# Attention and two expert mixtures on one core: second products of experts 1 to 4 of the first mixture in float32, straight from the staged weights

## The chip, the cores and the metric

The kernel runs on one core of a Trainium2 chip. Its time is the device time of one execution in microseconds (us). The comparison is the median of several runs of the kernel before and of the changed kernel on the same chip. The engines are named as the profile names them: PE is the matrix engine, PEld its weight loads, DVE the vector engine, ACT the activation engine, POOL the general engine (GpSimd), SP the queue that issues most transfers.

## The reference, cut to what matters

```python
def _moe_ref(x, w_gate, w1, w2):              # first mixture: N=3072, D=512, E=8, F=1024
    cap = N // E                              # 384 tokens for each expert
    logits = x @ w_gate
    # tokens are assigned greedily, the largest logit first, until an expert is full
    for e in range(E):
        mask = assigned == e
        h = np.maximum(x[mask] @ w1[e], 0.0)  # first product
        out[mask] = h @ w2[e]                 # second product
def reference(...):
    x = attention(q, k, v, mem_k, mem_v)      # local windows, 3072 tokens of 512
    x = _moe_ref(x, ...)                      # first mixture
    return _moe2_ref(x, ...)                  # second mixture: top 2 of 8 experts, noisy gate
```

## The kernel before, in words

After the attention the first mixture runs expert by expert. Two things go on at once. **The routing** decides which tokens an expert gets. It is a search, digit by digit, for the logit at which an expert is full, and each digit is a round trip between DVE and PE: DVE compares all tokens with some thresholds (tile `GE`), PE counts (`rps<-OH,GE`), DVE masks the counts (`blk`), PE adds them up (`rps<-blk,same`), DVE sums and compares with the capacity (`sums`, `flt`), PE sums the flags (`rps<-flt,onesb`), and DVE makes the next thresholds (`d`, `ci`, `GE`). One such round trip is called a pass below. An expert takes 8 passes and a closing part (`NQ`, `at`, `exc`, then the list of its tokens, `l1pos` and `slps`). **The experts** whose lists are ready are multiplied on PE in between. PE and DVE run their instructions in program order, and a planner (`Pipe`, with its own costs of instructions) has fixed that order when the program was built: routing products stand among the expert products.

An expert's tokens are gathered by POOL's indirect transfers (`xg<-xr,idx`) and transposed (`xT`). The first product (`mm1`) has 8 groups of 12 matmuls of 384 columns. Its weights come as float32 into staging tiles `st` (4 tiles of 128x1024 for each matrix, 8 buffers in all) and are split into float16 halves, a high and a low part: ACT takes squares for a scale (`junk<-st`) and writes the high part (`w_0h` to `w_3h`), and the low part (`w_0l` to `w_3l`) is made in `halves`, either by DVE in pieces of 256 columns or by POOL in pieces of 512 with two instructions (`st<-st,s`, then `w_0l<-st,w_0h`). The function asks DVE first (`fits`) and takes POOL when DVE has no room in the plan and POOL is idle (`idle`). Three float16 products stand for one product of float32. The rectified result of the first product is split likewise: ACT writes it twice (`ht` in float32, `hT` in float16) and POOL, or DVE, subtracts (`halve`, `hT<-ht,hT`). The second product (`mm2`) then takes 72 matmuls of 512 columns.

Expert 0 alone is done otherwise. ACT writes `hT` once, in float32, with the inverse scale of the first weights (`i1c`), and `mm2_f32` multiplies it with the staged float32 weights themselves: 48 matmuls of 256 columns in float32 into `m2f`. Its second weights are not split.

The transfers of weights are issued by SP in the order of `loads`: w1 of expert 0, w2 of expert 0, w1 of expert 1, and so on. Index i in the code is 2k for w1 and 2k+1 for w2 of expert k; experts 8 to 15 are those of the second mixture. `splits` takes the staged matrices in the same order. While a tile is in use its buffer can't be loaded again.

Of the kernel before, what the change touches and what calls it, by code (L numbers as in the profile page):

```python
# [25 lines left out]
KT, FT = DM // 128, FF // 128  # L26
# [948 lines left out]


C_H = 2.0**-15
SLACKG = -200.0

METAS = 8000.0  # L980
# [1 line left out]
SLACKH = 500.0  # L982


def loads(ctx):

    nc, pipe, t = ctx.nc, ctx.pipe, ctx.t
    for i in range(4 * E):
        k, m = i // 2, i % 2
        if k < E:  # L990
            yield lambda: k in ctx.est_known and (i < 2 or i == 3 or i - 2 in ctx.split)
            if m == 0:
                ev = pipe.D.value_load(ctx.est[0:1, k : k + 1], min_val=0, max_val=E - 1)
            elif k == 0:
                yield lambda: 0 in ctx.gathered
        else:
            yield lambda: i - 2 in ctx.split and (k == E or 1 in ctx.X2 and ctx.ordered)
            if m == 0 and k > E:
                ev = pipe.D.value_load(ctx.perm[0:1, k - E : k - E + 1], min_val=0, max_val=E - 1)
        if k < E:  # L1000
            yield ctx.split.get(i - 2, 0.0)
        else:
            pipe.t["y"] = max(pipe.t["y"], ctx.split[i - 2])
        got = ctx.st[i] = []
        for j in range(4):
            if i == 3:
                yield lambda: ctx.w2_read > 2 * j + 1
            st = ctx.stg.tile([128, 1024], F32, tag="st", name=f"st{i}_{j}", bufs=8)
            src = ((t.w1, t.w2) if k < E else (t.x1, t.x2))[m]
            if k == E:  # L1010
                src = src[0, j]
            else:
                src = src.rearrange("e j p n -> e p j n")[ds(ev, 1), :, j].rearrange("a p n -> (a p) n")
            pipe.D.dma_start(st, src)
            got.append(st)


def splits(ctx):

    for i in range(4 * E):
        if i == 1:
            continue
        yield lambda: i in ctx.st
        yield from split(ctx, i, ctx.st.pop(i), i == 0)


def split(ctx, i, st, eager):
    wp, pipe = ctx.wp, ctx.pipe
    V_, S_, G_ = pipe.V, pipe.S, pipe.G
    k, m = i // 2, i % 2
    W = ctx.W.setdefault(k, {"w1": [], "w2": []})

    def tl(n, shape=(128, 4), dt=F32, **kw):
        return wp.tile(list(shape), dt, tag=n, name=f"{n}_{i}", **kw)

    sq = tl("sq")  # L1040
    sqb = sq.bitcast(BF16).rearrange("p (j h) -> p j h", h=2)[:, :, 1]
    if m == 0:
        W["s1"], W["i1"] = tl("s1", dt=I32, bufs=3).bitcast(F32), tl("i1", dt=I32, bufs=3).bitcast(F32)
        if i == 0:
            W["i1c"] = tl("i1c", bufs=1)

    def after(x):
        return pipe.rdy("v", x) - 100

    def norms(js):  # L1050
        n = js.stop - js.start
        yield pipe.rdy("p", sq) + 1000
        tot = ctx.ms.tile([128, n], F32, tag="mso", name=f"tot{i}")
        pipe.P.matmul(tot, ctx.onesb, sqb[:, js], start=True, stop=True)
        t = tl("nt", dt=I32, bufs=1)
        yield pipe.rdy("v", tot) - 100
        V_.tensor_scalar(
            t[:, js], tot.bitcast(I32), 24, 23, op0=ALU.logical_shift_right, op1=ALU.logical_shift_left
        )
        yield after(t)  # L1060
        i2 = W["i1"] if m == 0 else tl("i2", dt=I32, bufs=1).bitcast(F32)
        V_.tensor_scalar(
            i2[:, js].bitcast(I32), t[:, js], float(23 << 23), float(50 << 23), op0=ALU.max, op1=ALU.add
        )
        if m == 0:
            yield after(i2)
            V_.tensor_scalar(
                W["s1"][:, js].bitcast(I32), i2[:, js].bitcast(I32), -1.0, float(254 << 23), op0=ALU.mult, op1=ALU.add
            )
            if i == 0:  # L1070
                V_.tensor_scalar(W["i1c"][:, js], W["i1"][:, js], C_H, None, op0=ALU.mult)
            return W["s1"]
        yield after(i2)
        q = tl("nq", dt=I32, bufs=1)
        V_.scalar_tensor_tensor(
            q, W["s1"].bitcast(I32), float(127 << 23), i2.bitcast(I32), op0=ALU.add, op1=ALU.subtract
        )
        yield after(q)
        kk = tl("kk", (128, 1), bufs=1)
        V_.tensor_reduce(kk, q.bitcast(F32), axis=AX.X, op=ALU.min)  # L1080
        yield after(kk)
        s2 = tl("s2")
        V_.tensor_scalar(s2, W["i1"], kk, None, op0=ALU.mult)
        comb = tl("comb", (128, 1), I32, bufs=3)
        V_.tensor_scalar(comb, kk.bitcast(I32), -1.0, float(254 << 23), op0=ALU.mult, op1=ALU.add)
        W["comb"] = comb.bitcast(F32)
        return s2

    def halves(j, s):
        done = W["w1" if m == 0 else "w2"]  # L1090
        n = 4 * (i - (i > 1)) + j
        yield lambda: ctx.wnext == n < len(ctx.wfree)
        ctx.wnext += 1
        hi, lo = (wp.tile([128, 1024], F16, tag=f"w{o}", name=f"w{i}_{j}{o}", bufs=12) for o in "hl")
        src = st[j]
        sj = s[:, j : j + 1]
        yield max(pipe.t["s"] - 100, pipe.rdy("s", s))
        pipe.t["s"] = max(pipe.t["s"], ctx.wfree[n] + 200)
        S_.activation(hi, src, AF.Copy, scale=sj)
        yield pipe.rdy("v", hi)  # L1100
        yield lambda: len(done) == j
        fits = pipe.fits(395.0)
        idle = lambda: k <= E and pipe.t["g"] <= pipe.clock + SLACKG
        a = 0
        while a < 1024:
            yield lambda: fits() or idle()
            b = a + 256 if fits() else min(a + 512, 1024)
            if b == a + 256:
                V_.scalar_tensor_tensor(lo[:, a:b], src[:, a:b], sj, hi[:, a:b], op0=ALU.mult, op1=ALU.subtract)
            else:  # L1110
                G_.tensor_scalar(src[:, a:b], src[:, a:b], sj, 1.0, op0=ALU.mult, op1=ALU.mult)
                G_.tensor_tensor(lo[:, a:b], src[:, a:b], hi[:, a:b], op=ALU.subtract)
            a = b
        kn = KT if m == 0 else 2
        hi, lo = (w.rearrange("p (k f) -> p k f", k=kn) for w in (hi, lo))
        done.append((hi, lo))
        if j == 3:
            ctx.split[i] = pipe.rdy("y", lo)

    for j in range(4):  # L1120
        if i == 0 and j > 1:
            yield lambda: 0 in ctx.X1
        yield lambda j=j: len(st) > j
        yield max(pipe.rdy("s", st[j]), pipe.t["s"] - 100)
        junk = ctx.junk.tile([128, 1024], F16, tag="junk", name=f"junk{i}_{j}")
        S_.activation(junk, st[j], AF.Square, accum_out=sq[:, j : j + 1])
        if eager:
            s = yield from norms(slice(j, j + 1))
            pipe.add(halves(j, s))
    if not eager:  # L1130
        s = yield from norms(slice(0, 4))
        if k < E:
            for j in reversed(range(4)):
                pipe.add(halves(j, s), True)
        else:
            for j in range(4):
                yield from halves(j, s)
# [15 lines left out]
def mm1(ctx, k, xT, n, ps, last=True):  # L1153

    pipe, W, hT = ctx.pipe, ctx.W[k], []
    for ft in range(FT):
# [15 lines left out]
                if i < 3 * KT:  # L1172
                    pipe.tick()
        h = ctx.hp.tile([128, 2, XN], F16, tag="hT", name="hT", bufs=FT + 1)
        if k == 0:
            h = h.rearrange("p o n -> p (o n)").bitcast(F32)[:, :n]
            pipe.S.activation(h, ps, AF.Relu, scale=W["i1c"][:, ft // 2 : ft // 2 + 1])
            hT.append(h)
# [37 lines left out]
    return ps  # L1216


def mm2_f32(ctx, hT):

    pipe = ctx.pipe
    ps = [ctx.m1.tile([128, DM], F32, tag="m1", name="m2f") for _ in range(CAP // 128)]
    pipe.until(lambda: 1 in ctx.st)
    for ft in range(FT):
        w2 = ctx.st[1][ft // 2].rearrange("p (k f) -> p k f", k=2)[:, ft % 2]
        pipe.wait(w2, hT[ft])
        for a in range(CAP // 128):
            for n in range(0, DM, DM // 2):
# [2 lines left out]
                    start=(ft == 0 and n == 0), stop=(ft == FT - 1 and n > 0),  # L1231
                )
                pipe.tick()
        ctx.w2_read = ft + 1
    ctx.split[1] = pipe.t["p"]
    return ps


# [160 lines left out]
def moe1(ctx):  # L1399
# [39 lines left out]
    for k in range(E):  # L1439
# [3 lines left out]
        hT = mm1(ctx, k, xT, CAP, ps)  # L1443
        m1_done.add(k)
        ys = ctx.wk.tile([128, NA], F32, tag="ys", name=f"ys{k}")
        if k:
            pipe.until(lambda: "comb" in ctx.W[k])
            pipe.V.tensor_scalar(ys, ix, ctx.W[k]["comb"], 1.0 / C_H, op0=ALU.mult, op1=ALU.mult)
        else:
            pipe.V.tensor_scalar(ys, ix, 1.0 / C_H, None, op0=ALU.mult)  # L1450
            f32 = mm2_f32(ctx, hT)
        for a in range(NA):
            ps = mm2(ctx, k, hT, 128 * a, last=a == NA - 1) if k else f32[a]
            y = ctx.xp.tile([128, DM], F32, tag="pv", name=f"y{k}{a}", bufs=8)
            pipe.S.activation(y, ps, AF.Copy, scale=ys[:, a : a + 1])
            ctx.Y[k, a] = y
# [244 lines left out]
def overflow(ctx):  # L1701
# [8 lines left out]
    with tc.For_i(0, total, 1):  # L1710
# [62 lines left out]
        ev = nc.sync.value_load(ei, min_val=0, max_val=E - 1)  # L1773
        k = 2 * E
        ctx.W.pop(k, None)
        ctx.wfree, ctx.wnext = [0.0] * (8 * (k + 1)), 8 * k - 4
        st = [[], []]
        for m, src in enumerate((t.x1, t.x2)):
            for j in range(4):
# [191 lines left out]
```

## Time and profile before

| | |
|---|---|
| median of 3 runs | 1163.11 us (1149.09 to 1164.64) |
| the profiled execution | 1158.95 us, of which its span 1157.1 us |
| PE busy | 993.3 us (86% of the span) |
| DVE busy | 777.3 us (67%) |
| ACT busy | 536.2 us (46%) |
| POOL busy | 566.4 us (49%) |
| mean granted clock of PE | 0.935 |

The span is the time from the first to the last instruction of the profiled execution; its own time lies 1.9 us above. A busy PE is not a PE at its peak: its records overlap, and a record is longer at a lower granted clock. The attention takes the first 190 us or so, the first mixture the next 390, the second mixture the rest.

### The profile page before, as it was taken

What the parts mean: (1) busy time and instruction counts of PE and PEld (TensorE: products, weight loads), DVE (VectorE), ACT (ScalarE), POOL (GpSimd) and SP (SyncE); (2) the same over time, 40 slices, a digit from 0 to 9 for tenths busy, and PEclk for the clock granted to TensorE, in tenths of its full rate; (3) what the DMA queues carried; (4) which work ended last, traced back from release to release, by engine and by line L of the source; (5) the groups of instructions that cost most, each with busy time, mean ns of one, the idle gap of its engine ahead of it and who ended that gap; (6) DMA issues with size and microseconds to landing.
All of it is one profiled execution on the core that took longest, in us unless ns stands there. A gap on an engine that the chain in (4) does not pass through costs nothing. (4 is left out here: it accounts for less than half of the span.)

```text
span 1157.1 us, 22131 instructions
## 1 busy us (share of the span) xinstructions
PE 993.3 (86%) x7959; PEld 556.4 (48%) x7959; DVE 777.3 (67%) x2352; ACT 536.2 (46%) x958; POOL 566.4 (49%) x690
## 2 busy tenths in 40 slices
PE   6677837987797888867978998999999999999995
PEld 6555635653343344433434554445455454555552
DVE  3576777879988989989677574654747365584100
ACT  2454514455564645667540862525536163553220
POOL 5455614436655656655553452544645445454531
PEclk9898857999997988989889998999999999999998
DMA  9999715528554554996524863665737476543410
GB/s 220 220 261 264 190 52 199 180 96 220 168 154 164 130 195 102 244 263 172 101 58 108 256 194 132 186 187 164 192 105 220 94 189 180 149 112 97 116 49 28
DMA packets 162660, 185.46 MB, mean 160 GB/s; under 512 B 108224, under 2 KB 120896, under 8 KB 162546
## 3 DMA queue, kind: packets, MB, share of 16 engines
q1 hardware_dynamic: 143856, 127.96, 42.5%
q0 software_dynamic: 15232, 49.75, 14.4%
q10 hardware_dynamic: 3458, 6.30, 1.5%
q8 instruction: 64, 1.05, 0.4%
q14 instruction: 50, 0.41, 0.1%
HBM read 127.14 MB, written 32.44 MB: 138 GB/s over the span
## 5 line engine op out<-in xcount | busy, mean ns | idle before, releaser
L68 PEld LDWEIGHTS <-hT 128*128 128x128 f16 (+2 forms) x2088 | 168.8, 99 | 196.9 <-issue 20.1
L68 ACT ACTIVATE ht<-m 128x384 f32<-128x384 f32 (+2 forms) x184 | 91.8, 499 | 330.8 <-PE m L68 302.0
L68 POOL TENSOR_TENSOR hT<-ht,hT 128x384 f16<-128x384 f32 (+2 forms) x154 | 153.3, 1007 | 134.4 <-ACT hT L68 122.1
L68 ACT ACTIVATE junk<-st 128x1024 f16<-128x1024 f32 x124 | 130.9, 1055 | 58.3 <-DMA st<-w_dram 31.3
L68 POOL DMA_INDIRECT out_dram<-pv,ts x47 | 47.1, 1003 | 179.2 <-DVE pv L68 117.8
L68 DVE SCALAR_TENSOR_TENSOR pv<-m,ys,pv 128x512 f32<-128x512 f32 (+2 forms) x47 | 33.5, 713 | 139.2 <-PE m L68 138.8
L68 PE MATMUL m<-xT,w_0h 128*128 128x384 f16 (+2 forms) x384 | 99.7, 339 | 3.3 <-DMA xT<-xg 3.3
L68 PE MATMUL m<-xT,w_1h 128*128 128x384 f16 (+2 forms) x384 | 102.5, 348 | 0.0
L68 PE MATMUL m<-xT,w_3h 128*128 128x384 f16 (+2 forms) x384 | 101.8, 344 | 0.0
L68 PE MATMUL m<-xT,w_2h 128*128 128x384 f16 (+2 forms) x384 | 99.3, 341 | 2.7 <-ACT hT L68 2.7
L68 PE MATMUL m<-w_3h,hT 128*128 128x512 f16 (+2 forms) x348 | 88.8, 353 | 5.6 <-POOL hT L68 5.6
L68 ACT ACTIVATE hT<-m 128x384 f16<-128x384 f32 (+2 forms) x184 | 91.4, 497 | 0.0
L68 PE MATMUL m<-w_0h,hT 128*128 128x512 f16 (+2 forms) x348 | 89.0, 360 | 0.0
L68 PE MATMUL m<-w_1h,hT 128*128 128x512 f16 (+2 forms) x348 | 87.9, 352 | 0.0
L68 PE MATMUL m<-w_2h,hT 128*128 128x512 f16 (+2 forms) x348 | 87.6, 350 | 0.0
L68 POOL TENSOR_SCALAR st<-st,s 128x512 f32<-128x512 f32 x63 | 53.9, 855 | 35.6 <-ACT w_0h L68 28.8
L68 DVE SCALAR_TENSOR_TENSOR w_1l<-st,s,w_1h 128x256 f16<-128x256 f32 x90 | 61.7, 725 | 13.2 <-ACT w_1h L68 13.2
L68 PE MATMUL m<-xT,w_1l 128*128 128x384 f16 (+2 forms) x192 | 67.4, 351 | 0.0
L68 POOL DMA_INDIRECT pv<-out_dram,tg x47 | 49.3, 1049 | 35.1 <-DVE xw L68 12.5
L68 PE MATMUL m<-xT,w_3l 128*128 128x384 f16 (+2 forms) x192 | 66.3, 345 | 0.0
L68 DVE SCALAR_TENSOR_TENSOR w_0l<-st,s,w_0h 128x256 f16<-128x256 f32 x90 | 54.4, 646 | 17.2 <-ACT w_0h L68 13.4
L68 PE MATMUL m<-xT,w_2l 128*128 128x384 f16 (+2 forms) x192 | 65.0, 338 | 0.0
(339 smaller groups left out, 2202.4 us busy)
## 6 DMA issues: line engine op xcount, KB each, us to landing
st<-w_dram SPq DMA_DIRECT2D x64, 512.0 KB, 6.2
st<-x_dram SPq DMA_DIRECT2D x64, 512.0 KB, 4.5
v<-vctx_dram SPq DMA_DIRECT2D x24, 520.0 KB, 14.9
k<-kT_dram SPq DMA_DIRECT2D x24, 312.0 KB, 15.6
x<-rb SPq DMA_DIRECT2D x24, 264.0 KB, 2.5
q<-qT_dram SPq DMA_DIRECT2D x12, 512.0 KB, 17.4
out_dram<-zero ACTq DMA_DIRECT2D x24, 256.0 KB, 2.3
xr<-rb POOLq DMA_DIRECT2D x17, 264.0 KB, 7.6
```

The costliest lines, as they stand in the source:

```text
L68: return f(*args, **kw)
```

## The change

The float32 way of expert 0 is taken by experts 0 to 4 (`KF = 5`). In these, w2 isn't split, `hT` is written once in float32, and the second product is 48 float32 matmuls instead of 72 float16 ones. Loads of w2 of expert k now wait until the second product of expert k-1 has read its tile (`w2_read`). And in the splitting of w1 of experts 1 to 4 POOL is no longer used when DVE has no room: the rule `idle` holds for expert 0 and for experts 5 to 8.

```diff
+KF = 5
+def whole(i):
+    return i % 2 == 1 and i // 2 < KF
+def order(i, j):
+    return 4 * (i - min(i // 2, KF)) + j
 def loads(ctx):
...
+        free = lambda: i < 2 or whole(i - 2) or i - 2 in ctx.split
         if k < E:
-            yield lambda: k in ctx.est_known and (i < 2 or i == 3 or i - 2 in ctx.split)
+            yield lambda: k in ctx.est_known and free()
...
         for j in range(4):
-            if i == 3:
-                yield lambda: ctx.w2_read > 2 * j + 1
+            if i > 1 and whole(i - 2):
+                yield lambda: ctx.w2_read > FT * (k - 1) + 2 * j + 1
...
 def splits(ctx):
     for i in range(4 * E):
-        if i == 1:
+        if whole(i):
             continue
...
-        idle = lambda: k <= E and pipe.t["g"] <= pipe.clock + SLACKG
+        idle = lambda: (k == 0 or KF <= k <= E) and pipe.t["g"] <= pipe.clock + SLACKG
...
-        if k == 0:
+        if k < KF:
             h = h.rearrange("p o n -> p (o n)").bitcast(F32)[:, :n]
             pipe.S.activation(h, ps, AF.Relu, scale=W["i1c"][:, ft // 2 : ft // 2 + 1])
...
-def mm2_f32(ctx, hT):
+def mm2_f32(ctx, k, hT):
...
-        w2 = ctx.st[1][ft // 2].rearrange("p (k f) -> p k f", k=2)[:, ft % 2]
+        pipe.until(lambda: len(ctx.st.get(2 * k + 1, ())) > ft // 2)
+        w2 = ctx.st[2 * k + 1][ft // 2].rearrange("p (k f) -> p k f", k=2)[:, ft % 2]
...
-            ps = mm2(ctx, k, hT, 128 * a, last=a == NA - 1) if k else f32[a]
+            ps = mm2(ctx, k, hT, 128 * a, last=a == NA - 1) if k >= KF else f32[a]
```

**PE, second product of expert 2.** Before, with a pass of the routing among the float16 matmuls (`m` is the result, `w_2h` and `w_2l` the halves):

```order
L68 MATMUL m_5166<-w_2h,hT 128x512
L68 LDWEIGHTS GE_5204
L68 MATMUL rps_5219<-OH_4878,GE_5204 120x64
L68 LDWEIGHTS GE_5204
L68 MATMUL rps_5219<-OH_4878,GE_5204 120x64
L68 LDWEIGHTS GE_5204
L68 MATMUL rps_5219<-OH_4878,GE_5204 120x64
L68 LDWEIGHTS hT
L68 MATMUL m_5166<-w_2h,hT 128x512
L68 LDWEIGHTS hT
L68 MATMUL m_5166<-w_2l,hT 128x512
```

The same place in the changed kernel (`st_0`, `st_1` are the staged float32 weights):

```order
L68 MATMUL m2f<-st_0_4371,hT 128x256 x4
L68 LDWEIGHTS GE_5009
L68 MATMUL rps_5020<-OH_4678,GE_5009 120x64
L68 LDWEIGHTS GE_5009
L68 MATMUL rps_5020<-OH_4678,GE_5009 120x64
L68 LDWEIGHTS GE_5009
L68 MATMUL rps_5020<-OH_4678,GE_5009 120x64
L68 MATMUL m2f<-st_0_4371,hT 128x256 x2
L68 LDWEIGHTS same
L68 MATMUL rps_5037<-blk_5024,same 15x64
L68 MATMUL m2f<-st_1_4440,hT 128x256 x3
```

A pass now has about 7 float32 matmuls beside it where it had about 13 float16 ones. Over experts 1 to 4 PE has 192 float32 matmuls more and 288 float16 ones fewer; 34 passes stand in their stretch instead of 32.

**POOL, behind the gather of expert 2.** Before, the splitting of w1 and w2 and the subtractions of `hT` up to the next gather:

```order
L68 COPY nz<-xg_2_4423 128x8
L68 TENSOR_SCALAR st_3_4159<-st_3_4159,s_4_4162 128x512
L68 TENSOR_TENSOR w_3l<-st_3_4159,w_3h 128x512
L68 TENSOR_TENSOR hT<-ht,hT 128x384
L68 TENSOR_SCALAR st_0_4406<-st_0_4406,s_5_4687 128x512
L68 TENSOR_TENSOR w_0l<-st_0_4406,w_0h 128x512
L68 TENSOR_SCALAR st_1_4408<-st_1_4408,s_5_4687 128x512
L68 TENSOR_TENSOR w_1l<-st_1_4408,w_1h 128x512
L68 TENSOR_SCALAR st_2_4410<-st_2_4410,s_5_4687 128x512
L68 TENSOR_TENSOR w_2l<-st_2_4410,w_2h 128x512
L68 TENSOR_TENSOR hT<-ht,hT 128x384 x4
```

In the changed kernel the gathers of experts 3 and 4 follow each other with copies of one and of eight columns alone:

```order
L68 COPY nz<-xg_2_4950 128x8
L68 DMA xg_0_5554<-xr,idx_83 128x528
L68 DMA xg_1_5556<-xr,idx_83 128x528
L68 DMA xg_2_5558<-xr,idx_83 128x528
L68 COPY ix_4_5536<-xg_0_5554 128x1
L68 COPY nz<-xg_0_5554 128x8
L68 COPY ix_4_5536<-xg_1_5556 128x1
L68 COPY nz<-xg_1_5556 128x8
L68 COPY ix_4_5536<-xg_2_5558 128x1
L68 COPY nz<-xg_2_5558 128x8
```

From the gather of expert 1 to that of expert 5 POOL has no arithmetic on weights or on `hT` any more. On DVE the number of pieces of 256 columns stays as it was, 16 for each of experts 1 to 4: all of w1, where it was 10 of w1 and 6 of w2.

**SP, the loads of w2 of expert 2.** Before they follow those of its w1 in one row, and the transposes of `xT` of expert 2 come behind them; in the changed kernel the four stand apart:

```order
L68 DMA st_0_4371<-w_dram 128x1024
L68 DMA_TRANSPOSE xT_4325<-xg_0_4341 128x8x128
L68 DMA_TRANSPOSE xT_4325<-xg_1_4343 128x8x128
L68 DMA_TRANSPOSE xT_4325<-xg_2_4345 128x8x128
L68 ISA
L68 DMA st_1_4440<-w_dram 128x1024
L68 ISA
L68 DMA st_2_4490<-w_dram 128x1024
L68 DMA_TRANSPOSE yT_4515<-rb_01_4079 128x8x128
```

Each of the four loads now stands where the second product of expert 1 has read two eighths more, with the transposes for the next expert and for the gate between them.

## Rows read from the trace of the kernel before

**Rows 1.** Windows: busy us (instructions) of PE, PEld, DVE, ACT, POOL; PEclk, DMA, GB/s.
```profile
242.00:444.00 202.00, 167.85 (x1042) 80.08 (x1042) 185.18 (x614) 110.86 (x197) 122.04 (x134) 0.92 0.55 159
444.00:583.00 139.00, 111.83 (x706) 57.23 (x705) 120.63 (x399) 88.26 (x160) 77.71 (x84) 0.91 0.70 179
713.00:1143.00 430.00, 423.09 (x2652) 222.53 (x2649) 216.30 (x529) 181.98 (x332) 201.90 (x202) 1.00 0.51 140
```

**Rows 2.** Timeline of PE: first matmuls of expert 1 and of expert 5.
```profile
242.16 0.50 PE L68 MATMUL m<-xT,w_0h 128*128 128x384 f16 x2
...
444.19 0.49 PE L68 MATMUL m<-xT,w_0h 128*128 128x384 f16 x2
```

**Rows 3.** PE's waits, 242-444 us: total us, times, longest; first, last of seven.
```profile
PE rps L68 <- DVE GE L68: 11.6, 8, 3.0
...
PE l1pos L68 <- DVE sure L68: 0.3, 1, 0.3
```

**Rows 4.** POOL's groups from 242 to 444 us: busy us, mean ns, idle before.
```profile
L68 POOL TENSOR_TENSOR hT<-ht,hT 128x384 f16<-128x384 f32 x32 | 33.7, 1059 | 60.3 <-ACT hT L68 60.3
L68 POOL TENSOR_SCALAR st<-st,s 128x512 f32<-128x512 f32 x33 | 28.5, 864 | 3.3 <-ACT w_0h L68 2.4 <-PE m L68 0.8
...
L68 POOL TENSOR_TENSOR w_3l<-st,w_3h 128x512 f16<-128x512 f32 x9 | 11.8, 1314 | 0.8
```

**Rows 5.** DVE's groups from 242 to 444 us, columns as in Rows 4.
```profile
L68 DVE SCALAR_TENSOR_TENSOR w_0l<-st,s,w_0h 128x256 f16<-128x256 f32 x16 | 13.4, 860 | 0.0
L68 DVE TENSOR_TENSOR flt<-sums,capB 15x8 bf16<-15x8 f32 x31 | 11.3, 363 | 1.1
...
L68 DVE TENSOR_TENSOR blk<-rps,own 120x64 f16<-120x64 f32 x32 | 6.9, 216 | 2.8 <-PE rps L68 2.5
```

**Rows 6.** DVE's timeline in expert 0's second product: start us, duration us.
```profile
233.67 0.47 DVE L68 SCALAR_TENSOR_TENSOR w_3l<-st,s,w_3h 128x256 f16<-128x256 f32 x1
...
236.15 0.22 DVE L68 TENSOR_TENSOR blk<-rps,own 120x64 f16<-120x64 f32 x1 [0.57 <-PE rps L68]
...
237.47 0.15 DVE L68 TENSOR_TENSOR flt<-sums,capB 15x8 bf16<-15x8 f32 x1
```

**Rows 7.** PE's timeline there, one pass (a float32 matmul leaves two records).
```profile
235.81 0.30 PE L68 MATMUL rps<-OH,GE 128*120 128x64 f16 x3
235.94 1.11 PE L68 MATMUL m2f<-st,hT 128*128 128x256 f32 x4
236.99 0.20 PE L68 MATMUL rps<-blk,same 120*15 120x64 f16 x1
237.11 1.13 PE L68 MATMUL m2f<-st,hT 128*128 128x256 f32 x4
238.18 0.17 PE L68 MATMUL rps<-flt,onesb 15*128 15x8 bf16 x1
238.28 1.56 PE L68 MATMUL m2f<-st,hT 128*128 128x256 f32 x6
239.68 0.30 PE L68 MATMUL rps<-OH,GE 128*120 128x64 f16 x3
```

**Rows 8.** PE's timeline, start and end of a pass in expert 2's second product.
```profile
326.10 0.35 PE L68 MATMUL rps<-OH,GE 128*120 128x64 f16 x3
...
329.54 0.30 PE L68 MATMUL rps<-OH,GE 128*120 128x64 f16 x3
```

**Rows 9.** Weight loads of tile m2f: ns min/median/max, first and last start.
```profile
L68 PEld LDWEIGHTS m2f<-st,hT x96: 186/190/192, 212.5 to 241.5; 128*128 128x128 f32 x96
```

**Rows 10.** PE's waits from 444 to 583 us, some of nine rows.
```profile
PE lg L68 <- DVE lg L68: 9.5, 4, 6.4
...
PE l1pos L68 <- DVE l1exc L68: 2.1, 1, 2.1
PE rps L68 <- DVE blk L68: 2.1, 1, 2.1
```

**Rows 11.** DMA issues: KB each, median us from issue to landing.
```profile
st<-w_dram SPq DMA_DIRECT2D x64, 512.0 KB, 6.2
```

More of the change, by code (lines that the diff above doesn't have):

```diff
@@ L996, in loads @@
         else:
-            yield lambda: i - 2 in ctx.split and (k == E or 1 in ctx.X2 and ctx.ordered)
+            yield lambda: free() and (k == E or 1 in ctx.X2 and ctx.ordered)
             if m == 0 and k > E:
@@ L1002, in loads @@
         else:
-            pipe.t["y"] = max(pipe.t["y"], ctx.split[i - 2])
+            pipe.t["y"] = max(pipe.t["y"], ctx.split.get(i - 2, 0.0))
         got = ctx.st[i] = []
         for j in range(4):
-            if i == 3:
-                yield lambda: ctx.w2_read > 2 * j + 1
+            if i > 1 and whole(i - 2):
+                yield lambda: ctx.w2_read > FT * (k - 1) + 2 * j + 1
             st = ctx.stg.tile([128, 1024], F32, tag="st", name=f"st{i}_{j}", bufs=8)
@@ L1043, in split @@
         W["s1"], W["i1"] = tl("s1", dt=I32, bufs=3).bitcast(F32), tl("i1", dt=I32, bufs=3).bitcast(F32)
-        if i == 0:
-            W["i1c"] = tl("i1c", bufs=1)
+        if k < KF:
+            W["i1c"] = tl("i1c", bufs=3)
     def after(x):
@@ L1069, in norms @@
             )
-            if i == 0:
+            if k < KF:
+                yield after(i2)
                 V_.tensor_scalar(W["i1c"][:, js], W["i1"][:, js], C_H, None, op0=ALU.mult)
@@ L1090, in halves @@
         done = W["w1" if m == 0 else "w2"]
-        n = 4 * (i - (i > 1)) + j
+        n = order(i, j)
         yield lambda: ctx.wnext == n < len(ctx.wfree)
@@ L1174, in mm1 @@
         h = ctx.hp.tile([128, 2, XN], F16, tag="hT", name="hT", bufs=FT + 1)
-        if k == 0:
+        if k < KF:
             h = h.rearrange("p o n -> p (o n)").bitcast(F32)[:, :n]
@@ L1216, in mm2 @@
     return ps
-def mm2_f32(ctx, hT):
+def mm2_f32(ctx, k, hT):
     pipe = ctx.pipe
     ps = [ctx.m1.tile([128, DM], F32, tag="m1", name="m2f") for _ in range(CAP // 128)]
-    pipe.until(lambda: 1 in ctx.st)
     for ft in range(FT):
-        w2 = ctx.st[1][ft // 2].rearrange("p (k f) -> p k f", k=2)[:, ft % 2]
+        pipe.until(lambda: len(ctx.st.get(2 * k + 1, ())) > ft // 2)
+        w2 = ctx.st[2 * k + 1][ft // 2].rearrange("p (k f) -> p k f", k=2)[:, ft % 2]
         pipe.wait(w2, hT[ft])
@@ L1233, in mm2_f32 @@
                 pipe.tick()
-        ctx.w2_read = ft + 1
-    ctx.split[1] = pipe.t["p"]
+        ctx.w2_read = FT * k + ft + 1
     return ps
@@ L1445, in moe1 @@
         ys = ctx.wk.tile([128, NA], F32, tag="ys", name=f"ys{k}")
-        if k:
+        if k >= KF:
             pipe.until(lambda: "comb" in ctx.W[k])
@@ L1450, in moe1 @@
             pipe.V.tensor_scalar(ys, ix, 1.0 / C_H, None, op0=ALU.mult)
-            f32 = mm2_f32(ctx, hT)
+            f32 = mm2_f32(ctx, k, hT)
         for a in range(NA):
-            ps = mm2(ctx, k, hT, 128 * a, last=a == NA - 1) if k else f32[a]
+            ps = mm2(ctx, k, hT, 128 * a, last=a == NA - 1) if k >= KF else f32[a]
             y = ctx.xp.tile([128, DM], F32, tag="pv", name=f"y{k}{a}", bufs=8)
@@ L1775, in overflow @@
         ctx.W.pop(k, None)
-        ctx.wfree, ctx.wnext = [0.0] * (8 * (k + 1)), 8 * k - 4
+        ctx.wfree, ctx.wnext = [0.0] * order(2 * k + 2, 0), order(2 * k, 0)
         st = [[], []]
```

## The prediction

> **What bounds the kernel now.** I read the page first: PE is busy for 86% of the span, so the question is where the rest lies. The windows tell it [rows 1]. From 713 to 1143 us PE is busy for 423 of 430 us at a granted clock of 1.00: the second mixture is bound by PE itself, and what comes earlier there ends earlier by as much. From 242 to 444 us, experts 1 to 4, PE is busy for 168 of 202 us at 0.92, and DVE for 185: both engines are nearly full, and neither is quite. These bounds are the experts' own: expert 1 begins at 242.16 us and expert 5 at 444.19 [rows 2].
>
> Next, PE's waits in this stretch [rows 3]. All seven rows name DVE, all of them are steps of the routing, and they sum to 33.5 us (the first is 11.6, the last 0.3). So PE stands in a queue behind a routing product whose input DVE hasn't made yet, and all expert products queue behind it. The lower clock costs too: 8% of the 168 us in which PE worked is 13.4 us. Without both, the four experts would take 202.0 - 33.5 - 13.4 = 155.1 us, or 38.8 each.
>
> Why is DVE late? Compare the same DVE instructions in two places. Between 233 and 242 us POOL does no arithmetic; there a piece of the low weights takes 0.47 us and `flt` 0.15 [rows 6]. From 242 to 444 us, where POOL splits weights and `hT`, the means are 860 ns for the pieces of `w_0l` and 363 ns for the 31 `flt` [rows 5]. `blk`, which reads its counts from the accumulators and has only one input beside them, takes 0.22 in either place [rows 5, 6]. So DVE's instructions are stretched while POOL computes, `flt` lies on the routing's chain, and PE waits at its end.
>
> **What POOL no longer does.** In this stretch POOL has 32 subtractions of `hT` (33.7 us), 33 scalings of staged weights (28.5 us) and as many subtractions after them, at about 1.3 us some 43 us: 105 of its 122 us [rows 1, 4]. The order of the changed kernel has none of these from the gather of expert 1 to that of expert 5; three gather issues and six small copies an expert are left. DVE's own work is the same to within a few small instructions (16 pieces an expert in both; the six of the norms of w2 go). ACT loses 8 long activations an expert and 8 writes of `ht`; it was busy for 111 of 202 us [rows 1] and on nobody's list of waits in rows 3, so this is worth nothing by itself. Nothing here lies on the path directly: its whole worth is that DVE keeps time.
>
> **What PE does more.** In expert 0 the float32 way can be read from the trace. A pass without any idle time of PE runs from 235.81 to 239.68 us and holds 14 records, that is 7 float32 matmuls: 3.87 us [rows 7]. 48 matmuls with their passes are 48/7 of it, 26.5 us, with 6.9 passes. A pass in the float16 product of expert 2, also without idle time, runs from 326.10 to 329.54 us with 13 matmuls beside it (by the order): 3.44 us [rows 8]. 72 matmuls are 72/13 of it, 19.0 us, with 5.5 passes. The difference is 7.5 us. 1.3 passes more are counted in the first number, while the stretch as a whole gets 34 passes for 32, or 0.5 an expert; the other 0.8 leave the first product, and at about 0.67 us a pass (3.44 less 13 matmuls of 512 columns at 2.4 GHz, 2.77 us) that is 0.5 back. **The price is 7.0 us an expert, 28 us in all.** It is paid on the path, and nothing hides it, since PE then has no idle time there.
>
> One rule of the Trainium skill speaks against this. In the trace the weight loads of the float32 matmuls take 186 ns [rows 9], and 14 of them are 2.6 us of the pass of 3.87 us; they lie beside the matmuls, or the pass would be longer. "TensorE: Matmul & The Clock Gate", section "Weight-path perf modes", says that the fast weight load brings no gain for fp32. If the loads couldn't be hidden, an estimate by the row would be 2.6 us more in a pass, 18 us more an expert, and the sum would be 1211 us. The pass in rows 7 already holds them, so the sum goes by the pass.
>
> **The stage after.** 38.8 + 7.0 = 45.8 us an expert, 183 for the four, if PE never waits and the clock stays at its upper level. The nearest rows for the waits are those of expert 0's quiet part, where PE has none over the whole pass and DVE waits for PE instead, 0.57 us before `blk` [rows 6, 7]. The other end is that all 8.4 us an expert stay. I take 1.3 us an expert for waits and clock together, near the quiet end: gathers and copies still come from POOL, and the closing part of a routing step is denser on DVE than a pass. That makes 188.5 us instead of 202.0: **13.5 us gained**, between 18.8 gained and 28 lost.
>
> **Around it.** Expert 5 also gets rid of the last two passes and the closing part of the routing, which the changed order has inside expert 4; its waits for `l1exc` and `blk` (2.1 us each) go with them [rows 10]. I put 4.5 us on this, passes included. Experts 5 to 7 keep POOL and their splitting; PE waits there for the gate's `lg` (9.5 us) because DVE is behind [rows 10]. DVE enters the stretch with less arrears, and the clock is 0.91 there [rows 1]; between 5 us lost and 10 gained I take 2 gained, nearer to no change, as their own work stays.
>
> **Edits with one answer.** The four loads of w2 move on SP's queue to where PE has read the tile's predecessor. Queued behind each are transposes of `xT` and of the gate rows, the former for an expert that begins some 20 us later; a load lands in 6.2 us [rows 11], so even a load held up by that much costs nothing. If the queue were stuck for a whole second product, the next expert would start late by some 6 us each. w2 itself has nearly a whole expert's time to land. `i1c` for four experts is one small DVE instruction each.
>
> The sum: 1158.95 - 13.5 - 4.5 - 2 = **1139 us**. The profiled execution lies 4 us below the median of 1163.11 and inside its spread, so I let the number stand for the median as well; 2% of it, about 23 us, is what a measurement of this kernel can tell from no change.
>
> **The rivals.** *The routing itself is the bound* (slower). If PE waits because the round trip is long, not because POOL stretches it, then the 33.5 us and the slow clock stay while PE pays 28 us: 1187 us. For it speaks that DVE is busy for 185 of 202 us; against it the quiet pass of rows 7. It decides for slower from the point where more than 18.8 us of the 46.9 us of waits and lost clock remain. *The gain is eaten by expert 5.* Its w2 is the first to be split again, and can be loaded only when expert 4's second product has read the tiles; its norm product stands behind 56 of 96 matmuls of the first product in the order, where before it stood at the start. Squares, the high halves and 16 pieces then have some 12 us before PE needs the last of them. The 16 pieces alone are 7.5 us at 0.47, but 13.8 at 0.86 [rows 5, 6]. If ACT or DVE can't keep that, PE waits 5 to 10 us there, and arrears go on through experts 6 and 7: about 1150 us. *The gain is larger.* Without any waits the four experts give 18.8, and if DVE's arrears don't reach experts 5 to 7, the 10 us come in: 1158.95 - 18.8 - 4.5 - 10 = 1126, and a few us more if expert 0, beside which w1 of expert 1 is split without POOL too, loses its own waits: 1124 us. *The change doesn't do what it says*: DVE has no room for the pieces POOL gave up, and w1 of the next expert comes late. The order has them all on DVE; its work then is 16 x 0.47 = 7.5 us an expert plus the routing, which I hold to fit. This would show as waits of PE for weights and give some 1160 us.
>
> **How the numbers follow.** Forecast, 1128 to 1150 around 1139: 0.50. Larger gain, about 1124: 0.22. Eaten by expert 5 or not as said, 1150 to 1163: 0.21. Routing is the bound, up to 1187: 0.07. The range leaves out half of the last and the lowest end of the larger gain: 1117 to 1165. Faster by over 2% are the larger gain and a little under half of the forecast, 0.44; slower by over 2% only the far part of the last rival, 0.04; within 2% is the rest, 0.52.
>
> **What would show it.** Right: from expert 1 to expert 5 about 188 us; PE's waits there under 8 us in all, its granted clock near 1.00; DVE's pieces near 0.47 us and `flt` near 0.15; a pass in the second products near 3.9 us. Wrong: waits of PE for `GE`, `flt` or `blk` as before, or waits for weights at the second product of expert 5. The number is wrong if the stages are as said and the time isn't: then something between 444 and 713 us has taken the gain back.

## The result and the profile after

| | before | changed |
|---|---|---|
| median | 1162.36 us (1149.09 to 1164.64, 4 runs) | 1120.58 us (1119.61 to 1121.97, 4 runs) |
| profiled execution | 1158.95 us | 1120.83 us |

The ratio is 0.9669, with an interval of 0.9633 to 0.9706: faster by some 3.3%, and 18 us below the forecast of 1139 us. Ratios, here and below, are of undisturbed executions; one execution of a variant below, at 1211.56 us and a granted clock of 0.82, is left out of its median too. The page of the changed kernel begins so (busy us and share of the span; x instructions):

```profile
span 1119.0 us, 21999 instructions
...
PE 1000.2 (89%) x8051; PEld 598.2 (53%) x8051; DVE 730.9 (65%) x2337; ACT 495.0 (44%) x878; POOL 461.3 (41%) x589
```

PE's timeline of the changed kernel gives the bounds of the stage, the first matmuls of expert 1 and of expert 5 (start us, duration us; the row of [rows 2]):

```profile
238.11 0.50 PE L68 MATMUL m<-xT,w_0h 128*128 128x384 f16 x2
...
421.49 0.33 PE L68 MATMUL m<-xT,w_0h 128*128 128x384 f16 x1
```

Experts 1 to 4 take 183.4 us where they took 202.0. From the same kind of row for every expert, the span divides as follows (first matmul of one to first matmul of the next, us):

| stretch | before | changed | difference |
|---|---|---|---|
| up to expert 0 | 192.7 | 191.6 | -1.1 |
| expert 0 | 49.5 | 46.5 | -3.0 |
| experts 1 to 4 | 202.0 | 183.4 | -18.6 |
| expert 5 | 44.7 | 40.2 | -4.5 |
| expert 6 | 46.2 | 35.6 | -10.6 |
| expert 7 | 48.1 | 48.7 | +0.6 |
| second mixture | 573.9 | 573.0 | -0.9 |

The windows of the changed kernel, columns as in [rows 1] (the first is experts 1 to 4, then experts 5 to 7, then the quiet part of the second mixture):

```profile
238.00:421.00 183.00, 179.54 (x1191) 122.41 (x1191) 150.51 (x677) 71.71 (x122) 26.88 (x44) 1.00 0.69 183
421.00:546.00 125.00, 107.95 (x650) 55.28 (x649) 106.45 (x318) 87.67 (x160) 69.92 (x78) 0.92 0.71 192
675.00:1105.00 430.00, 423.91 (x2661) 222.95 (x2655) 218.53 (x529) 182.25 (x332) 200.68 (x201) 1.00 0.51 140
```

In the first stretch PE is busy for 179.5 of 183 us, the granted clock is 1.00 where it was 0.92, POOL has 26.9 us of work for 122, and DVE's busy time falls by 35 us although its instructions are more (677 for 614). The third stretch is what it was. PE's waits in the first stretch, all of them (total us, times, longest), where those of [rows 3] sum to 33.5:

```profile
PE rps L68 <- DVE GE L68: 2.3, 4, 0.9
PE rps L68 <- DVE flt L68: 0.6, 1, 0.6
PE rps L68 <- DVE blk L68: 0.5, 1, 0.5
```

No wait for weights is among them: the four loads of w2 that were moved behind transposes always landed in time. DVE's groups from 238.1 to 421.5 us (busy us, mean ns | idle before), beside [rows 5]:

```profile
L68 DVE TENSOR_TENSOR blk<-rps,own 120x64 f16<-120x64 f32 x34 | 7.5, 222 | 7.5 <-PE rps L68 7.2
...
L68 DVE SCALAR_TENSOR_TENSOR w_0l<-st,s,w_0h 128x256 f16<-128x256 f32 x14 | 6.4, 474 | 0.0
...
L68 DVE TENSOR_TENSOR flt<-sums,capB 15x8 bf16<-15x8 f32 x35 | 5.6, 161 | 1.2
```

A piece of `w_0l` takes 474 ns for 860 (over the pieces of all four tiles the means are 491 and 686), `flt` 161 for 363, `blk` 222 for 216, and DVE now idles 7.2 us ahead of `blk` for PE, where it idled 2.5. POOL's groups of the same time, beside [rows 4], have gathers, their copies and four pairs of splitting left, all for w1 of expert 5:

```profile
L68 POOL DMA_INDIRECT xg<-xr,idx x12 | 12.4, 1031 | 128.4 <-issue 93.1 <-DVE ci L68 35.2
...
L68 POOL TENSOR_SCALAR st<-st,s 128x512 f32<-128x512 f32 x4 | 3.2, 790 | 1.3 <-ACT w_0h L68 1.3
```

A pass in the second product of expert 1 on PE's timeline (two records for a float32 matmul, as in [rows 7]):

```profile
262.93 0.30 PE L68 MATMUL rps<-OH,GE 128*120 128x64 f16 x3
263.07 1.11 PE L68 MATMUL m2f<-st,hT 128*128 128x256 f32 x4
264.11 0.20 PE L68 MATMUL rps<-blk,same 120*15 120x64 f16 x1
264.23 1.13 PE L68 MATMUL m2f<-st,hT 128*128 128x256 f32 x4
265.30 0.17 PE L68 MATMUL rps<-flt,onesb 15*128 15x8 bf16 x1
265.40 1.99 PE L68 MATMUL m2f<-st,hT 128*128 128x256 f32 x8
267.23 0.30 PE L68 MATMUL rps<-OH,GE 128*120 128x64 f16 x3
```

It holds 16 records, 8 matmuls, in 4.30 us, so 7 would take 3.76 (forecast 3.87). No idle time stands at any of the three routing products: the answer of DVE is there before PE reaches them.

At the second product of expert 5, the first whose weights are split again, PE does wait, as one rival said, but for less (PE's timeline, idle time and releaser in brackets):

```profile
441.40 0.59 PE L68 MATMUL m<-w_0h,hT 128*128 128x512 f16 x2 [2.94 <-ACT w_0h L68]
443.48 0.59 PE L68 MATMUL m<-w_0l,hT 128*128 128x512 f16 x1 [1.48 <-POOL w_0l L68]
```

### The profile page after: what moved, and what is told of

Read it like the earlier page. It is cut to its first block, busy times and chain, and to the rows that moved or that the text cites. A ratio compares the mean times of both kernels' runs of the same rounds, so it can differ in the third digit from the quotient of the medians.

```text
span 1119.0 us, 21999 instructions
## 1 busy us (share of the span) xinstructions
PE 1000.2 (89%) x8051; PEld 598.2 (53%) x8051; DVE 730.9 (65%) x2337; ACT 495.0 (44%) x878; POOL 461.3 (41%) x589
## 5 line engine op out<-in xcount | busy, mean ns | idle before, releaser
L68 PEld LDWEIGHTS <-hT 128*128 128x128 f16 (+2 forms) x1800 | 144.6, 100 | 183.4 <-issue 22.6
L68 ACT ACTIVATE ht<-m 128x384 f32<-128x384 f32 (+2 forms) x152 | 76.3, 502 | 255.0 <-PE m L68 230.6
L68 ACT ACTIVATE junk<-st 128x1024 f16<-128x1024 f32 x108 | 114.1, 1056 | 62.2 <-DVE sloh L68 22.6
L68 POOL TENSOR_TENSOR hT<-ht,hT 128x384 f16<-128x384 f32 (+2 forms) x121 | 117.2, 980 | 55.3 <-ACT hT L68 40.1
L68 DVE SCALAR_TENSOR_TENSOR pv<-m,ys,pv 128x512 f32<-128x512 f32 (+2 forms) x47 | 33.5, 714 | 148.5 <-PE m L68 148.1
L68 PE MATMUL m2f<-st,hT 128*128 128x256 f32 x480 | 124.7, 396 | 0.0
L68 POOL DMA_INDIRECT xg<-xr,idx x24 | 24.8, 1032 | 186.7 <-issue 95.4
L68 PEld LDWEIGHTS m2f<-st,hT 128*128 128x128 f32 x480 | 84.4, 190 | 10.0 <-ACT hT L68 0.3
L68 PE MATMUL m<-w_3h,hT 128*128 128x512 f16 (+2 forms) x300 | 72.5, 347 | 8.4 <-POOL hT L68 8.4
L68 PE MATMUL m<-xT,w_0l 128*128 128x384 f16 (+2 forms) x192 | 64.5, 336 | 0.0
L68 DVE SCALAR_TENSOR_TENSOR w_2l<-st,s,w_2h 128x256 f16<-128x256 f32 x102 | 61.9, 657 | 3.5 <-ACT w_2h L68 3.5
```

Of the source, the lines that this page charges most:

```text
L68: return f(*args, **kw)
```

## The experiments

The theory under test: PE waited in experts 1 to 4 because POOL's arithmetic stretched DVE's instructions, and the change pays since it takes that arithmetic away; the float32 product is its price on PE. Against it stood that the gain comes from PE's order or from fewer matmuls, whatever POOL does. Each run has its own kernel before on the same chip; ratios are to that.

**One half of the change: float32 products, with POOL free to split w1.**

```diff
-        idle = lambda: (k == 0 or KF <= k <= E) and pipe.t["g"] <= ...
+        idle = lambda: k <= E and pipe.t["g"] <= ...
```

> The changed kernel with one part undone: POOL may again help to split w1 of experts 1 to 4 (3 pairs of instructions an expert in the order, 6 DVE pieces fewer). Theory (POOL's arithmetic stretches DVE's instructions, and PE waits for DVE): some 6 us of POOL arithmetic an expert where the kernel before had 26 and paid 11.7 us an expert in waits and clock, so up to 2.8 us an expert: 1123 to 1133 us. Rival (the gain comes from the work that ACT and DVE lost with w2 and from float32, and POOL does no harm): 1117 to 1122 us, since DVE has 6 pieces an expert less.

1140.91 us, ratio 0.9848 (0.98 to 0.9896): a worse result than the theory's range, and the rival fell. Windows and PE's waits of this kernel for experts 1 to 4:

```profile
243.30:436.30 193.00, 182.08 (x1202) 122.47 (x1202) 157.29 (x670) 70.69 (x123) 50.85 (x65) 1.00 0.65 179
```

```profile
PE rps L68 <- DVE flt L68: 5.2, 6, 1.6
PE rps L68 <- DVE blk L68: 2.7, 5, 0.7
PE rps L68 <- DVE GE L68: 2.3, 6, 0.5
```

POOL has 24 us more of work than in the changed kernel, and the stretch takes 193.0 us for 183.4, within what was expected of it. Expert 0 takes 49.4 us, as before the change, and expert 6 40.4; these two, 2.9 and 4.8 us more than in the changed kernel, are most of what the expectation left out.

**The other half: the kernel before, with POOL kept from splitting weights in experts 1 to 4.** Here that means w1 and w2 alike, since w2 is still split.

```diff
-        idle = lambda: k <= E and pipe.t["g"] <= ...
+        idle = lambda: (k == 0 or 5 <= k <= E) and pipe.t["g"] <= ...
```

> The kernel before with the other part alone: second products in float16 as before, but POOL splits no weights of experts 1 to 4; DVE makes all 32 pieces an expert, and POOL keeps the subtractions of hT. Theory: POOL falls from 122 to about 50 us in the stretch, DVE's stretching by about two thirds, but DVE takes 16 pieces more an expert, 7.5 us at 0.47; the two nearly cancel, DVE stays as full as before: 1135 to 1158 us. Rival (keeping POOL off the weights is the whole of the gain, float32 only a detail): at or below 1125 us.

1172.48 us, ratio 1.0118 (1.0074 to 1.0161): slower by 1.2%, and both expectations fell. Windows, first waits of PE and one of DVE's groups for experts 1 to 4, three views of this kernel:

```profile
239.70:474.50 234.80, 173.80 (x1136) 87.68 (x1136) 211.29 (x819) 122.91 (x216) 63.92 (x87) 0.86 0.60 168
```

```profile
PE rps L68 <- DVE GE L68: 23.9, 15, 4.2
PE rps L68 <- DVE flt L68: 13.2, 16, 1.2
PE rps L68 <- DVE blk L68: 6.6, 15, 1.4
```

```profile
L68 DVE SCALAR_TENSOR_TENSOR w_0l<-st,s,w_0h 128x256 f16<-128x256 f32 x32 | 16.7, 543 | 0.0
```

A piece is cheap here, 543 ns, but DVE has 132 of them over the four tiles where the changed kernel has 56 in its stretch, and it is busy for 211 of 235 us. So POOL's share can't just be handed to DVE while w2 is split too. The halves don't add: -18.8 us for the first alone (from the 1159.71 us of before in these runs), +12.8 for the second, about -40 together. Float32 is worth its price on PE because it takes away work that POOL or DVE would otherwise have to do.

**POOL's load put back into the changed kernel.** POOL does as much arithmetic as before on scratch tiles that nobody reads; the order on PE, DVE and ACT stays that of the changed kernel.

```diff
+        for c, n in ((0, 384), (384, 384), (768, 256)) if 0 < k < KF else ():
+            z, y = (... tag="ht" ... for _ in "zy")
+            ctx.nc.gpsimd.tensor_scalar(z, src[:, c : c + n], sj, 1.0, op0=ALU.mult, op1=ALU.mult)
+            ctx.nc.gpsimd.tensor_tensor(y, z, hi[:, c : c + n], op=ALU.subtract)
...
+            if k:
+                ctx.nc.gpsimd.tensor_tensor(z, h, h, op=ALU.subtract)
```

> The changed kernel with POOL's load put back: for experts 1 to 4 POOL subtracts each float32 hT tile from itself and makes scaled copies and differences of all columns of w1, into scratch tiles that nobody reads; the plan isn't told, so the order on PE, DVE and ACT stays that of the changed kernel. POOL's arithmetic in the stretch is then about the 105 us of the kernel before. Theory: pieces of 256 columns go back to 0.6 to 0.9 us and flt to about 0.35, PE's waits to between half and all of 33.5 us, the clock falls again: 1140 to 1167 us. Rival (gain from ACT's and DVE's lost work): 1118 to 1126 us.

1146.74 us, ratio 0.989 (0.9861 to 0.9919), as the theory had it. Windows, waits of PE and groups of DVE for experts 1 to 4 of this kernel:

```profile
244.80:451.50 206.70, 186.59 (x1193) 122.58 (x1193) 187.17 (x679) 71.71 (x122) 119.10 (x153) 0.99 0.60 163
```

```profile
PE rps L68 <- DVE GE L68: 8.4, 13, 1.4
PE rps L68 <- DVE flt L68: 4.8, 11, 0.8
PE rps L68 <- DVE blk L68: 3.9, 7, 0.7
```

```profile
L68 DVE TENSOR_TENSOR flt<-sums,capB 15x8 bf16<-15x8 f32 x35 | 9.8, 279 | 1.2
L68 DVE SCALAR_TENSOR_TENSOR w_0l<-st,s,w_0h 128x256 f16<-128x256 f32 x14 | 9.5, 693 | 0.0
...
L68 DVE TENSOR_TENSOR blk<-rps,own 120x64 f16<-120x64 f32 x34 | 7.3, 216 | 3.5 <-PE rps L68 2.4 <-PE m L68 1.0
```

With the same instructions in the same order on PE, DVE and ACT, the 92 us that POOL has more than in the changed kernel cost 23.3 us: `flt` goes from 161 to 279 ns, a piece of `w_0l` from 474 to 693, `blk` stays, and PE waits 19 us for DVE where it waited 3.4. No wait for weights is on PE's list, although POOL's scratch work reads the staged tiles too. The other 7 us are PE's own busy time, 186.6 us for 179.5. Two parts of the expectation failed: the clock stayed at 0.99, and `flt` stayed below 350 ns.

"SBUF — State Buffer" of the Trainium skill, section "Who interferes with whom", has the shared port pair of DVE and GpSimd as the only point of contention among the engines, an exclusive lock. The trace agrees as far as it goes: `flt` and the pieces, which read two tiles in SBUF, are stretched, and `blk`, which takes its counts from the accumulators, isn't. That the port is the cause, and that it is locked, no run here shows.

**POOL's work taken out of the kernel before.** It's still planned (`account`), but not issued: the low halves that POOL would make are left out, and PE reads the high half in their place (`kept`). PE's order and the number of its matmuls stay those of before.

```diff
+                if 0 < k < 5:
+                    pipe.account("g", "tensor_scalar", ...)
...
+                    LEFT_OUT.add(lo.tensor.name)
+                else:
+                    G_.tensor_scalar(src[:, a:b], ...)
+                    G_.tensor_tensor(lo[:, a:b], ...)
...
-                    ps, w1[wo][:, kt, fs], xT[:, KT * xo + kt, :n], ...
+                ctx.nc.tensor.matmul(ps, kept(w1, wo)[:, kt, fs], x, ...)
```

> The kernel before, with POOL's arithmetic of experts 1 to 4 left out and the plan unchanged: pieces of low weights and low halves of hT that POOL would make aren't made, and PE reads the high half in their place, in the same number of matmuls; so part of the low-order terms of the products is replaced by wrong ones. It costs what the work would cost if another engine had it for nothing. Theory: PE's 33.5 us of waits and 13.4 us of slow clock in experts 1 to 4 nearly vanish, float32's price isn't paid, and expert 6 gains as in the changed kernel: 1098 to 1118 us. Rival (the routing's round trip or the plan is the bound): above 1150 us.

1108.01 us, ratio 0.9556 (0.9506 to 0.9606); the rival fell. Windows and waits for experts 1 to 4 of this kernel:

```profile
239.00:394.70 155.70, 151.01 (x1041) 76.81 (x1042) 136.86 (x615) 110.36 (x197) 27.39 (x44) 1.00 0.70 206
```

```profile
PE rps L68 <- DVE flt L68: 1.8, 2, 1.0
PE rps L68 <- DVE GE L68: 1.3, 5, 0.4
PE rps L68 <- DVE blk L68: 1.2, 1, 1.2
```

46.3 us less in this stretch, with 1041 instructions of PE for the 1042 of [rows 1]. Routing and matmuls of the kernel before fit beside each other; it was POOL's work that kept them apart. Expert 0 takes 46.9 us here, so the 3.0 us of expert 0 come from POOL too, which split w1 of expert 1 there. Expert 5, where POOL computes again and the last passes of the routing stand in this order, takes 49.0 us for 44.7: the gain of experts 1 to 4 doesn't reach beyond them here.

**How many experts.** One size is changed, to 3, 7 and 8 float32 experts; the rule `idle` moves with it, so that POOL also splits no weights of experts 1 to `KF` - 1:

```diff
-KF = 5
+KF = 3
```

> The changed kernel with KF = 3: experts 0 to 2 in float32, 3 and 4 as before (POOL splits and subtracts there). Theory: experts 1 and 2 take about 46 us as in the changed kernel, 3 and 4 about 51 as before, and DVE is behind again when expert 6 needs its gate rows: 1120.6 + 2 x 5.5 for experts 3 and 4, and 0 to 10 us for expert 6: 1130 to 1143 us. Rival (the gain hangs on the routing being finished within expert 4, all or nothing): above 1150 us.

> The changed kernel with KF = 7: experts 5 and 6, beside which no routing runs, in float32 as well, POOL off their weights. Their products cost PE 5 us more each than in float16 and have no passes beside them; what there is to gain are waits and slow clock, some 7 us in expert 5 (4.4 us of waits for w2, clock 0.92) and 3 us in expert 6. Theory: 1116 to 1128 us, no clear change. Rival (float32 pays wherever POOL's arithmetic goes): at or below 1112 us.

> The changed kernel with KF = 8, the whole first mixture in float32. Expert 7 takes 48.7 us in the changed kernel with 9 us of waits for lists and gate rows and a clock of 0.86; if POOL's arithmetic is behind these too, up to 10 us come off for 5 us of float32. Theory: 1110 to 1126 us. Rival (those waits are DVE's own chain of gate and lists): 1122 to 1132 us.

Three: 1140.77 us, ratio 0.9806 (0.9743 to 0.9868). Seven: 1123.76, 0.9669 (0.9604 to 0.9733). Eight: 1119.87, 0.9643 (0.9577 to 0.9708). All lie where the theory had them. Beyond the experts beside which the routing runs, no further gain is seen. That is the sum of two things, since POOL is taken off more weights as well: the next kernel has five float32 experts and the same rule `idle` as the one with eight, and ran on the same chip in 1114.37 us, 5.5 us less. So float32 in experts 5 to 7 seems to cost more than it spares, though the two intervals overlap; five and six experts under that rule, further below, differ in the same direction.

**No POOL for the splitting in experts 5 to 7 either.** KF is 5 again:

```diff
-        idle = lambda: (k == 0 or KF <= k <= E) and ...
+        idle = lambda: (k == 0 or k == E) and ...
```

> The changed kernel, and POOL off the weights of experts 5 to 7 as well, whose second products stay in float16 with split weights; POOL keeps their hT. In experts 1 to 4 of the kernel before the same step alone made DVE the bound; here no routing runs, so DVE has some 20 us an expert free. Theory: 18 pairs of POOL instructions go, DVE takes 36 pieces more, 17 us in all over three experts with 106 us of DVE in 125: no clear change, 1114 to 1128 us. Rival (POOL's stretching is always worse than DVE's own work): at or below 1112 us.

1114.37 us, ratio 0.9605 (0.9542 to 0.9668), at the lower end of what was expected and not told apart from the changed kernel by its interval. So it ran again beside it, with two neighbours: one with `idle` for expert 0 alone, one with `KF = 6` on top of the line above.

> The changed kernel itself, on the same chip as the next three, so that a variant can be set against it. Theory: about 1120 us, ratio to the kernel before near 0.967. There is no rival; it is the yardstick.

> The changed kernel with POOL's splitting of weights kept to expert 0 and to the first expert of the second mixture, so that experts 5 to 7 are split by DVE alone. It ran once at 1114.37 us. Theory (DVE in experts 5 to 7 is also stretched by POOL, and spares more without it than the extra pieces cost): 1110 to 1117 us, at least 3 us below the changed kernel of the same call. Rival (chance of one program): within 3 us of the changed kernel.

> As the run before it, but POOL splits weights for expert 0 alone; the first expert of the second mixture goes to DVE too. Theory: a further 0 to 4 us less, 1108 to 1116 us, since that stretch still shows DVE's pieces at over 1 us. Rival: DVE has no room there (list work for the second mixture), PE waits for weights, and the time rises to 1116 to 1130 us.

> As the run of five experts without POOL in experts 5 to 7, but the second products of six experts in float32 (KF = 6). In expert 5 no routing stands any more, so that a float32 second product costs PE 26.5 us where the float16 one took 20. Theory: DVE is spared 16 pieces of 0.5 to 1 us there, but PE is the bound in expert 5 and pays 4 to 7 us: 1114 to 1121 us, at or above the run of five experts. Rival (DVE still sets the pace in experts 5 to 7): 1105 to 1112 us.

The changed kernel: 1123.86 us, ratio 0.9659 (0.9623 to 0.9695). Without POOL in experts 5 to 7: 1113.0, 0.9579 (0.9552 to 0.9605). With POOL for expert 0 alone: 1111.44, 0.9562 (0.9519 to 0.9604). With six experts: 1116.1, 0.9613 (0.9578 to 0.9647). The second is faster than the changed kernel by about 1%, and the intervals don't meet, so that the expectation of no clear change fell with the repetition; the third and the fourth can't be told from the second, and all three lie where the theory had them. Of the second's 10.9 us the profiled executions place 4.6 behind the start of expert 0; where the rest lies is open. Windows and pieces of DVE from expert 5 to the second mixture's second expert, first of the changed kernel in this group of runs:

```profile
425.30:601.90 176.60, 149.34 (x934) 76.48 (x933) 145.59 (x434) 104.90 (x193) 91.04 (x97) 0.91 0.62 170
```

```profile
L68 DVE SCALAR_TENSOR_TENSOR w_2l<-st,s,w_2h 128x256 f16<-128x256 f32 x26 | 22.1, 902 | 0.0
L68 DVE SCALAR_TENSOR_TENSOR w_1l<-st,s,w_1h 128x256 f16<-128x256 f32 x16 | 13.6, 890 | 0.0
...
L68 DVE SCALAR_TENSOR_TENSOR w_0l<-st,s,w_0h 128x256 f16<-128x256 f32 x14 | 12.2, 896 | 3.7 <-ACT w_0h L68 2.5 <-issue 1.2
L68 DVE SCALAR_TENSOR_TENSOR w_3l<-st,s,w_3h 128x256 f16<-128x256 f32 x16 | 8.3, 563 | 0.0
```

and of the one without POOL in experts 5 to 7:

```profile
418.60:591.40 172.80, 150.41 (x1068) 82.28 (x1067) 133.31 (x445) 99.63 (x185) 69.62 (x77) 0.96 0.60 159
```

```profile
L68 DVE SCALAR_TENSOR_TENSOR w_2l<-st,s,w_2h 128x256 f16<-128x256 f32 x26 | 12.8, 537 | 0.0
L68 DVE SCALAR_TENSOR_TENSOR w_0l<-st,s,w_0h 128x256 f16<-128x256 f32 x24 | 12.1, 545 | 5.2 <-ACT w_0h L68 5.2
L68 DVE SCALAR_TENSOR_TENSOR w_3l<-st,s,w_3h 128x256 f16<-128x256 f32 x24 | 11.4, 507 | 0.0
...
L68 DVE SCALAR_TENSOR_TENSOR w_1l<-st,s,w_1h 128x256 f16<-128x256 f32 x22 | 9.5, 478 | 0.0
```

DVE makes more pieces (over the four tiles 96 for 72) and is busy for 12 us less. The pieces are stretched here as in experts 1 to 4, in a place that the change left alone.

**Expert 6.** No run was made for it, but two of those above bear on it. Windows and PE's waits there, of the changed kernel with POOL's load put back in experts 1 to 4:

```profile
491.20:526.90 35.70, 32.36 (x197) 17.04 (x196) 30.54 (x78) 31.53 (x61) 20.29 (x20) 1.00 0.68 214
```

```profile
PE m L68 <- ACT hT L68: 1.7, 1, 1.7
```

and of the kernel before with POOL's work of experts 1 to 4 left out:

```profile
443.70:488.50 44.80, 34.54 (x220) 18.19 (x219) 38.90 (x126) 31.87 (x62) 21.65 (x26) 0.92 0.84 227
```

```profile
PE lg L68 <- DVE lg L68: 9.0, 3, 6.9
```

After disturbed experts 1 to 4, with the changed order: 35.7 us. After undisturbed ones, with the order of before: 44.8. Before the change it was 46.2. So the 10.6 us of expert 6 come with the order, and at most 1.4 of them from arrears that DVE brings along from experts 1 to 4. DVE has 78 instructions in expert 6 for 126, and a count by tile shows what is gone: of the gate's arithmetic (tiles `gw`, `gd`, `gq`, `gu`, `glw`, `gny`, `gm`, `ge`, `goh`, `gmx`) experts 5, 6 and 7 have 27, 11 and 16 instructions in the changed kernel, and had 0, 34 and 20 before. Half of it has moved ahead into expert 5, which the routing has left, and PE's products for `lg` no longer wait for DVE in expert 6, where they waited 8.5 us. Arrears out of expert 5 itself aren't ruled out as a part of those 8.5 us: in the run with the order of before PE still waits 8.2 us for the routing there.

## Why the prediction was right or wrong, point by point

**What bounds the stage** was right. That DVE is late because POOL computes is shown from both sides: POOL's work put back costs 23.3 us, and taken out of the kernel before gives 46.3. The slower rival, that the round trip itself is the bound, fell with these two runs.

**38.8 us an expert without waits** was 1.0 too high. Without POOL the kernel before has PE busy for 151.0 us, not 155.1. The clock is not what was off. Between 242 and 444 us it stood at its lower level (0.50) for 30.7 us in all, and PE was busy for 27.8 of these, which costs 13.9 us where I took 13.4. But PE's busy time fell by 16.8 us with its order unchanged, so 2.9 us of it are neither idle time nor clock, and 0.6 us of idle time are on no row of the list of waits. What failed, in the main, is that I priced a wait at its idle time alone. With POOL's load put back the same shows: 7 us more of PE's busy time for the same matmuls, of which 1.7 are clock (3.4 us at the lower level). A reason that fits, not tested by itself: in the kernel before a float16 matmul of 512 columns starts 0.21 us behind another (327.60 and 327.81 us), while its record lasts 0.38, so PE counts as busy for up to 0.17 us longer, an estimate, wherever the next one isn't there in time.

**The price of 7.0 us** was right: 179.5 us of busy PE for 151.0 at the same clock is 28.5 us for four experts, 7.1 each. The second products took 26.5, 26.3, 25.5 and 26.6 us (forecast 26.5). The 480 weight loads of `m2f` still take 190 ns and stay hidden, so the case in which they show, 1211 us, didn't come.

**1.3 us an expert for waits and clock** should have been 0.85: 3.4 us of waits in all and no lost clock. The other end that I set beside it was wrong: 8.4 us an expert are the waits alone, and it is 11.7 with the clock that makes the 28 us lost. Together with the term above that makes 18.6 us gained for 13.5; the bound of 18.8 was nearly reached.

**4.5 us in expert 5** was met, in sum. In it are 4.4 us of new waits for split weights, so the rival in which expert 5 eats the gain has its mechanism in the trace, a little below its 5 to 10 us, and without arrears in expert 6 behind it.

**2 us from experts 5 to 7** is the term that failed most: 10.0 us came, the very end that I had named for it, but not for the reason named, so this agreement is luck in good part. I took their work as unchanged and asked only for DVE's arrears, while half of the gate's work moved from experts 6 and 7 into expert 5. The order of expert 6 was in front of me, and I hadn't counted DVE's instructions in it.

**Expert 0** was left out of the sum, and named in the larger-gain rival alone; it gave 3.0 us. By place, the 18 us between forecast and result are 5.1 in experts 1 to 4, 8.0 in experts 5 to 7, 3.0 in expert 0 and 2.0 outside them. The likeliest case, 1128 to 1150 us, was too cautious, and what came was the larger gain, which had 0.22, even a little below its 1124 us and in part by other means than it named.

**The loads of w2 cost nothing**, as forecast: no wait for them is on PE's list.

**What remains open:** by which of its rules the planner moves the gate's work was not followed. Of the 8.8 us between the spans of the last comparison (1121.9 and 1113.1 us), 4.2 lie in the attention, ahead of expert 0, which neither version touches: expert 0 began at 191.6 and at 195.4 us in two profiled executions of the changed program itself. From expert 0 on the better version is ahead by 4.6 us (3.9 in the earlier pair of executions), while the medians differ by 10.9; the rest of that isn't found in these two executions.

## What to carry to other kernels

When the engine that closes a round trip has small instructions that take twice their quiet time, ask first who else computes at that time, and compare the same instruction in a quiet place; work given to an idle neighbour may cost more on the chain than it spares. A product that costs more on the bound engine can pay if it removes the preparation that disturbs the chain, and then both halves of the edit are needed. Where a change moves a planner's order, count the instructions of every stage behind the edit too: here expert 6 alone gave 10.6 us, beside the 18.6 aimed at.

## What the runs showed of the hardware that I had not expected

DVE can spend less time on all of a work than on the part that POOL leaves it: 96 pieces with POOL off the weights of experts 5 to 7 kept DVE busy for 45.8 us (12.8 + 12.1 + 11.4 + 9.5), 72 with POOL splitting the others for 56.2 (22.1 + 13.6 + 12.2 + 8.3).

Waits don't always lower the clock. With POOL's load put back PE was idle for 20 of 207 us, in many short gaps, and the granted clock was 0.99; in the kernel before it was idle for 34 of 202 at 0.92, and with only the splitting taken from POOL for 61 of 235 at 0.86.

A wait costs PE more than the idle time that the profile gives for it: with POOL's load put back PE's busy time grew by 7 us besides the 16 us of additional waits, at a clock of 0.99.
